# Four raw weight buffers instead of three, and weights joined straight into their buffers, in a fused attention and two-MLP kernel

## The chip, the cores and the metric

The kernel runs on one core of a Trainium2 chip. The metric is the device time of one execution, in microseconds (us). Engines are named as in the profile: PE (TensorE, matmuls), DVE (VectorE), ACT (ScalarE), POOL (GpSimd) and SP (SyncE, which only issues transfers). Each engine works through its own instructions in order.

## What is computed

The weights come out of `setup_inputs` in float64, since they are scaled by a float64 factor; q, k and v are float32. Cut to what matters:

```python
# q, k, v: (4, 8, 576, 64); chunks of 64
scores = scale * q_c @ k_c^T            # per chunk, 64 x 64
attn = softmax(scores); out = attn @ v_c
x = out as 2304 tokens x 512
h = x @ w_in                            # 512 x 2048
x = silu(h) @ w_out                     # 2048 x 512
a, b = x @ w_a, x @ w_b                 # 512 x 1536 each
return (a * b) @ w_out2                 # 1536 x 512; w_o in the kernel
```

## The kernel before

**Weights.** The kernel receives the float64 weights as 64-bit words and makes float32 of them on the chip. There are 68 units of 128 x 512 words (512 KB each): 32 "a" units (`w_in` and `w_out`, 16 each, for the first MLP) and 36 "b" units (`w_a`, `w_b`, `w_o`, 12 each, for the second). One conversion has four steps, each a function: `fetch` (SP transfers the words into a raw buffer, L143), `magnitude` (DVE clamps the high words, L165), `scaled` (ACT makes two passes over the raw buffer, L176 and L178), and `begin` (DVE joins high and low words into a tile `w`, L188, and so frees the raw buffer). The raw buffers are used in turn; there are `RAWS = 3`. `convert` (named "cv" in the orders below) calls `fetch_next` and then `scaled`; `joined` ("af") calls `begin` and then `magnitude`. `fetch_next` issues one fetch if a buffer is free, and then `leave` issues the stores of finished `w` tiles, on SP too.

A joined "a" unit is split into a high part (`upper`, ACT, L210) and a low part (`lower`, DVE, L217), because each product is made of three matmuls in a rounded format (high x high, high x low, low x high). `w_out` units are also stored to HBM (`wo`). A joined "b" unit is stored to HBM as `wf` (36 stores of 256 KB).

**First MLP.** `front` is x @ `w_in` for one of 16 slices m of the hidden width (12 matmuls of 512 columns, then SiLU twice on ACT into `g` and `ghi`, L418, and their difference `glo` on DVE, L416); `back` adds the slice's product with `w_out`. The loop `for k in range(MA)` (the first pass, k = 0 to 15) runs over the slices for the first block of tokens and, beside it, for a side block of 256 tokens, while the weights of the slice after it are converted. The order of the instructions in one iteration is a list of words written out by hand, with "cv" and "af" three times each. The second pass (k = 16 to 31) runs the slices for the second block, with "cv" and "af" twice per iteration; its attention tiles belong to the blocks of the group stage. Then comes the group stage, 32 products `g_front` for the last two blocks, each followed by `g_silu`, and behind them seven rounds of `g_back`.

Attention tiles are spread over the iterations: scores, maximum, exponential, norm, transposes and values of a tile are each put at a fixed word of some iteration. In the first pass four tiles start at k = 2, 5, 8 and 11; scores come at the tile's first iteration, transposes two later and values three later.

**Second MLP.** It uses products of blocks in the manner of Strassen (seven instead of eight), so its weights need sums. The sums for ten units (`w_a`/`w_b` units 0 to 3, and the six `w_o` units) are made ahead ("premade"): `comb_load` and `comb_load_2` bring a unit's two parts from `wf` into a slot `buf` (POOL transfers), `comb_sums` makes the sums (DVE: one of 256, one of 512, one of 256 columns), `comb_high` (ACT) and `comb_low` (DVE) split them, and POOL stores the result (`wg`, `w2`). They are taken from the list `aux_ops`, one step per iteration of the second pass from k = 25 on ("au"), two per product of the group stage. The other eight units are loaded from `wf` and summed later, during the second MLP itself.

**Memory.** The pool `big` has `MA + 4` = 20 slots of 8 KB per partition, for weights, inputs, outputs, `buf` and the split parts. Transfers issued by POOL take their descriptors from a scratch in SBUF; it has 16 KB per partition where the program names no other size.

Of the kernel before, what the change touches and what calls it, by code (L numbers as in the profile page):

```python
# [9 lines left out]
F32 = mybir.dt.float32  # L10
F32R = mybir.dt.float32r
U32 = mybir.dt.uint32
# [4 lines left out]
ALU = mybir.AluOpType  # L17
# [11 lines left out]
def chunk_attention_silu_mlp_gated_mlp(  # L29
# [67 lines left out]

    const = ctx.enter_context(tc.tile_pool(name="const", bufs=1))
    stat = ctx.enter_context(tc.tile_pool(name="stat", bufs=3))
    big = ctx.enter_context(tc.tile_pool(name="big", bufs=MA + 4))  # L100
    gpool = ctx.enter_context(tc.tile_pool(name="gpool", bufs=2))
    spool = ctx.enter_context(tc.tile_pool(name="spool", bufs=2))
    dram = ctx.enter_context(tc.tile_pool(name="dram", bufs=1, space=DRAM))
# [11 lines left out]
        return big.tile([P, 4 * DM], dt, tag="b", name=name)  # L115


    RAWS = 3
    def raw_tile():
        return spool.tile([P, RAWS, DM], U64, tag="raw", name="raws", bufs=1)  # L120

# [30 lines left out]
    def words(raw):  # L152
        w32 = raw.bitcast(U32).rearrange("p (f t) -> p f t", t=2)
        return w32[:, :, 0], w32[:, :, 1]
# [26 lines left out]
    def begin():  # L181

        if not opened:
            return
        dest, raw = opened.pop(0)
        low, high = words(raw)
        w = spool.tile([P, DM], F32, tag="tmp", name="w", bufs=3)
        nc.vector.scalar_tensor_tensor(  # L188
            out=w.bitcast(U32), in0=high, scalar=3, in1=low,
            op0=ALU.logical_shift_left, op1=ALU.bitwise_or,  # L190
        )
        if dest[0] == "f":
            wf[dest[1:]] = d = dram.tile([P, DM], F32, name=f"wf{dest[1]}{dest[2]}")
            leaving.append((d, w))
        else:
            _, m, j = dest
            if j:
                w2h = w.rearrange("p (h n) -> p h n", h=2)
                leaving.append((wo[:, m % 2, :, m // 2], w2h))
            stage_1.append((dest, w))  # L200
# [275 lines left out]
            nc.gpsimd.dma_start(out=buf[:, sl], in_=wf[mat, m].rearrange("p (o n) -> p o n", o=2))  # L476
        bufs[u] = buf

    def comb_load_2(s):

        buf = slot("buf", F32).rearrange("p (o n) -> p o n", o=8)
        for h in range(2):
            nc.gpsimd.dma_start(out=buf[:, 1 - h], in_=wf[2, 2 * s][:, h * H:(h + 1) * H])
        nc.gpsimd.dma_start(
            out=buf[:, 2:8:5], in_=wf[2, 2 * s + 1].rearrange("p (o n) -> p o n", o=2)
        )
        bufs["o", s] = buf

    summed = set()

# [147 lines left out]
        ]  # L638


    units_a = [(m, j) for m in range(MA) for j in range(2)]
    units_b = []
    for s in range(STEPS):
        for mat in range(2):
            units_b += [("f", mat, 2 * s), ("f", mat, 2 * s + 1), ("f", 2, 2 * s + mat)]
    done = [0, 0]

    def next_a():
# [18 lines left out]
    with tc.manual_schedule():  # L667
# [325 lines left out]
        def g_take(s, y):  # L993

            if s == 0:
                g_units[s, y] = [
                    gpool.tile([P, DM], F32R, tag=tg, name="u") for tg in ("ghi", "glo")
                ]
                return
            if y and s > 2:  # L1000
                t = late["gun"].tile([P, 2, DM], F32R, tag=f"u{s}", name="u")
                g_units[s, y] = t[:, 0], t[:, 1]
            elif s < 3 or s > 5:
                if (s, y) not in g_units:
                    t = slot("u").rearrange("p (u t n) -> p u t n", u=2, t=2)
                    pair = ((s, 0), (s, 1)) if s < 3 else ((6, 0), (7, 0))
                    for i, key in enumerate(pair):
                        g_units[key] = t[:, i, 0], t[:, i, 1]
            elif (s, y) not in g_units:
                t = spool.tile([P, 6, DM], F32R, tag="raw", name="u", bufs=1)  # L1010
                for i in range(3):
                    g_units[3 + i, 0] = t[:, 2 * i], t[:, 2 * i + 1]

        def g_front(n):
            m, h = divmod(n, 2)
# [143 lines left out]

        def fetch_next():  # L1160

            if len(fetched) + len(opened) < RAWS:
                fetches[0] += 1
                if done[0] < len(units_a) and fetches[0] % 3:
                    fetch(*next_a())
                elif done[1] < len(units_b):
                    fetch(*next_b())
            leave()

        def convert():  # L1170
# [27 lines left out]
        }  # L1198
        for k in range(MA):
            run(k, "x")  # L1200
            for x in order:
                if x in todo_1:
                    todo_1[x](k)
                else:
                    run(k, x[0])
            run(k, "e")

        aux = [("o", 0), ("o", 1), ("o", 2), 0, ("o", 3), 1, ("o", 4), 2, ("o", 5), 3]

        def aux_load():  # L1210
            if aux:
                u = aux.pop(0)
                (comb_load if u in range(UNITS) else lambda u: comb_load_2(u[1]))(u)
                aux_ops.extend(((comb_sums, u), (comb_high, u, 0), (comb_low, u, 0, 1), (comb_low, u, 1)))

        aux_ops = []

        def comb_high(u, h):
            o0, o1 = HALVES[h]
# [21 lines left out]
        def aux_op():  # L1241
            if not aux_ops:
                return
            f, *args = aux_ops.pop(0)
            if f is comb_sums:
                aux_load()
            f(*args)

        AUX_FROM = MA + 9

        def next_front(k):
            if k + 1 == END:
# [2 lines left out]
            elif k + 1 not in pend:  # L1255
                front(k + 1)

        def aux_step(k):
            if k == AUX_FROM:
                aux_load()  # L1260
            elif k > AUX_FROM:
                aux_op()

        order_2 = (
            "fr a a2 cv c fi af d au ba cv b e af"
        ).split()
        todo_2 = {
            "fr": next_front,
            "cv": lambda k: convert(),
            "af": lambda k: joined(),  # L1270
            "fi": lambda k: finish(pend, k + 1),
            "au": aux_step,
            "ba": lambda k: k in pend and back(k),
        }

# [3 lines left out]
        for k in range(MA, END):  # L1279
            b, m = steps[k]  # L1280
            run(k, "x")
            if k == MA:
                side_cm.__exit__(None, None, None)
                g_cm = tc.tile_pool(name="gate", bufs=1, side="right", reuse_waits="tile")
                late["g"] = g_cm.__enter__()
            for x in order_2:
                if x in todo_2:
                    todo_2[x](k)
                else:
                    run(k, x)  # L1290

        for n, g in enumerate([0, 2, 4, 6, 1, 3, 5, 7] + list(range(8, 4 * SA))):
            if n > 1:
                g_front(g)
            if n == 2:
                run(END, "a")
            if n == 4:
                late.pop("g")
                g_cm.__exit__(None, None, None)
                att_cm.__exit__(None, None, None)  # L1300
                gun_cm = tc.tile_pool(name="gun", bufs=1, side="right", reuse_waits="tile")
                late["gun"] = gun_cm.__enter__()
            g_silu(g)
            if fetched or opened or leaving:
                convert()
                joined()
            if n > 3:
                aux_op()
                aux_op()
            if n == 4 * SA - 12:  # L1310
                w_load("a11")
            if n >= 4 * SA - 3:
                w_chunk(0, n - (4 * SA - 3))
            if n == 4 * SA - 2:
                w_load("a12")
# [260 lines left out]
```

## Time and profile before

| | |
|---|---|
| median of 3 runs | 856.1 us (853.99 to 857.77) |
| the profiled execution's own time | 859.48 us |
| its span, first to last instruction | 857.7 us |
| PE busy | 832.2 us, 97% |
| DVE busy | 550.0 us, 64% |
| ACT busy | 468.4 us, 55% |
| POOL busy | 65.4 us, 8% |
| data moved | 209.59 MB, 244 GB/s in the mean |

Busy time is the time in which an engine executes; waits for other engines are not in it. The profiled execution is one execution, not the median; 1.8 us of its own time lie outside the span.

### The profile page before, as it was taken

Reading aid. Unit: us, or ns where it says so; the run is one execution under the profiler, and the core shown is the slowest. Engines: PE = TensorE matmul, PEld = TensorE weight load, DVE = VectorE, ACT = ScalarE, POOL = GpSimd, SP = SyncE. Lnnn points to the kernel's source line nnn. Section 1 sums busy time; section 2 is a strip of 40 time slices with the busy share of each in tenths; the row PEclk is TensorE's granted clock in tenths of the full one; section 3 lists DMA queues with packets and bytes.
Section 4 is the critical chain, followed back from the end, with each engine's and each line's share of the span. In section 5 each row is a group of like instructions: output and inputs, shape, how many; then the busy total and the mean of one; then the engine's idle time right before and its main releaser. Section 6 shows DMA issues by size and latency. Waiting matters only on the chain.

```text
span 857.7 us, 14083 instructions
## 1 busy us (share of the span) xinstructions
PE 832.2 (97%) x5394; PEld 757.8 (88%) x5394; DVE 550.0 (64%) x972; ACT 468.4 (55%) x900; POOL 65.4 (8%) x118
## 2 busy tenths in 40 slices
PE   7989799898999999999999999999999999999998
PEld 6878688776888888888889999999999999999998
DVE  5656566566763567789885998594454594454563
ACT  6967677767885544465664554373333273333252
POOL 1000000001022123310001110000000000000000
PEclk8999999999999999999999999999999999999999
DMA  8577577779872449982039977888666888666761
GB/s 297 163 233 236 204 244 240 223 253 339 287 256 75 160 160 309 328 316 89 12 106 371 380 304 285 328 300 292 246 254 250 301 339 264 241 252 255 291 236 55
DMA packets 58083, 209.59 MB, mean 244 GB/s; under 512 B 6432, under 2 KB 18336, under 8 KB 48544
## 3 DMA queue, kind: packets, MB, share of 16 engines
q1 hardware_dynamic: 47264, 169.07, 54.8%
q0 software_dynamic: 10464, 39.33, 13.4%
q8 instruction: 42, 0.69, 0.3%
q10 hardware_dynamic: 288, 0.30, 0.1%
q14 instruction: 25, 0.20, 0.1%
HBM read 152.57 MB, written 56.10 MB: 243 GB/s over the span
## 4 chain that ended last, share of the span: by engine, by line
PE 80%; DMA 9%; ACT 5%; DVE 3%; issue 2%; SPq 0%; POOL 0%; DVEq 0%; ACTq 0%
PE ps_acc L897 26%; PE ps_sA L897 8%; PE ps_mm L897 8%; PE ps_sB L897 7%; PE ps_at L897 7%; PE ps_acc L436 6%; DMA raws<-w_out 5%; PE ps_acc L390 5%; PE ps_mm L390 5%; PE ps_sA L390 3%; PE ps_at L390 2%; DMA raws<-w_o 2%; PE ps_sB L390 1%; DVE w L188 1%; ACT raws L178 1%
## 5 line engine op out<-in xcount | busy, mean ns | idle before, releaser
L897 PE MATMUL ps_acc<-xo,ring 128*128 128x384 f32 x902 | 171.9, 334 | 0.0
L897 PEld LDWEIGHTS ps_acc<-xo,ring 128*128 128x128 f32 x902 | 157.7, 188 | 0.4 <-DVE gq L972 0.3
L436 PE MATMUL ps_acc<-ghi,wA 128*128 128x512 f32 x256 | 84.2, 411 | 6.1 <-ACT ghi L418 4.9
L176 ACT ACTIVATE raws<-raws 128x512 int32<-128x512 uint8 x68 | 46.8, 689 | 34.0 <-DMA raws<-w_out 24.9
L390 PE MATMUL ps_mm<-xhi,wA 128*128 128x512 f32 x224 | 61.6, 397 | 0.2
L188 DVE SCALAR_TENSOR_TENSOR w<-raws 128x512 uint32<-128x512 uint32 x68 | 46.8, 689 | 23.0 <-ACT raws L178 21.2
L897 PE MATMUL ps_acc<-u,ring 128*128 128x384 f32 x322 | 61.3, 334 | 0.0
L436 PEld LDWEIGHTS ps_acc<-ghi,wA 128*128 128x128 f32 x256 | 46.8, 194 | 16.4 <-ACT ghi L418 6.2
L1344 ACT ACTIVATE u<-gq 128x384 fp32r<-128x384 f32 x84 | 40.6, 517 | 30.9 <-DVE gq L972 28.5
L897 PEld LDWEIGHTS ps_acc<-u,ring 128*128 128x128 f32 x322 | 56.3, 188 | 0.0
L1345 DVE TENSOR_TENSOR u<-gq,u 128x384 fp32r<-128x384 f32 x84 | 44.4, 552 | 15.2 <-ACT u L1344 15.0
L178 ACT ACTIVATE raws<-raws 128x512 f32<-128x512 f32 x68 | 45.5, 669 | 11.9 <-DVE raws L165 11.7
L436 PE MATMUL ps_acc<-glo,wA 128*128 128x512 f32 x128 | 51.6, 403 | 0.0
L390 PEld LDWEIGHTS ps_mm<-xhi,wA 128*128 128x128 f32 x224 | 40.9, 190 | 8.0 <-PE ps_sB L436 0.6
L165 DVE TENSOR_SCALAR raws<-raws 128x512 f32<-128x512 f32 x68 | 28.8, 423 | 28.4 <-DMA raws<-w_out 21.7
L416 DVE TENSOR_TENSOR glo<-g,ghi 128x512 fp32r<-128x512 f32 (+1 forms) x48 | 28.7, 598 | 26.2 <-ACT ghi L418 26.1
L897 PE MATMUL ps_sA<-xo,ring 128*128 128x384 f32 x220 | 44.4, 334 | 0.0
L906 ACT ACTIVATE gq<-ps_acc 128x384 f32<-128x384 f32 x31 | 15.3, 492 | 52.8 <-PE ps_acc L897 49.7
L897 PE MATMUL ps_mm<-xo,ring 128*128 128x384 f32 x214 | 43.2, 334 | 0.0
L897 PE MATMUL ps_sB<-xo,ring 128*128 128x384 f32 x208 | 42.3, 335 | 0.0
L897 PE MATMUL ps_at<-xo,ring 128*128 128x384 f32 x202 | 41.0, 334 | 0.0
L897 PEld LDWEIGHTS ps_sA<-xo,ring 128*128 128x128 f32 x220 | 38.7, 188 | 0.0
(250 smaller groups left out, 1742.6 us busy)
## 6 DMA issues: line engine op xcount, KB each, us to landing
ring<-w SPq DMA_DIRECT2D x30, 1024.0 KB, 6.4
ring<-wg SPq DMA_DIRECT2D x28, 1024.0 KB, 4.9
ring<-wg SPq DMA_DIRECT2D x28, 768.0 KB, 6.0
wf<-w SPq DMA_DIRECT2D x36, 256.0 KB, 3.7
raws<-w_in SPq DMA_DIRECT2D x16, 512.0 KB, 4.8
raws<-w_out SPq DMA_DIRECT2D x16, 512.0 KB, 4.5
wg<-ring SPq DMA_DIRECT2D x8, 1024.0 KB, 4.6
buf<-wf POOLq DMA_DIRECT2D x26, 256.0 KB, 6.1
```

Source lines behind the costliest of these rows:

```text
L165: nc.vector.tensor_scalar(out=high, in0=high, scalar1=LARGEST, scalar2=-LARGEST, op0=ALU.min, op1=ALU.max)
L176: nc.scalar.activation(low.bitcast(I32), top, AF.Copy, scale=2.0**-5, bias=-31 / 64)
L178: nc.scalar.activation(high, high, AF.Prelu, scale=2.0**-112, alpha=-(2.0**32))
L188: nc.vector.scalar_tensor_tensor(out=w.bitcast(U32), in0=high, scalar=3, in1=low, op0=ALU.logical_shift_left, op1=ALU.bitwise_or,)
L390: nc.tensor.matmul(ps, lhsT=a[:, kk * P:(kk + 1) * P], rhs=b[:, kk, :], start=(j == 0 and kk == 0), stop=(j == 2 and kk == KT - 1),)
L416: nc.vector.tensor_tensor(out=glo, in0=g, in1=ghi.bitcast(F32), op=ALU.subtract)
L436: nc.tensor.matmul(acc_t[b][j], lhsT=a[:, j * P:(j + 1) * P], rhs=g, start=(m == 0 and i == 0 and (b != SIDE or j % 2 == 0)), stop=(m == M ...
L897: nc.tensor.matmul(ps, lhsT=a, rhs=b, start=first and i == 0, stop=last and i == 2, skip_group_check=True,)
L906: nc.scalar.activation(dst, ps, AF.Copy)
L1344: nc.scalar.activation(hi, src, AF.Copy)
L1345: nc.vector.tensor_tensor(out=lo, in0=src, in1=hi.bitcast(F32), op=ALU.subtract)
```

## The change

A fourth raw buffer and a 21st slot are paid for with the POOL scratch, cut from 16 KB to 4 KB per partition (a raw buffer is 4 KB, a slot 8 KB). `fetch_next` may issue two fetches at a call. Every fourth iteration of the first pass leaves its third "cv" and "af" out, the second pass has one of each per iteration instead of two, and products 2 to 19 of the group stage have one each. The 20 "b" units of the premade sums come last in the order of conversion, and `begin` writes them with two joins of 256 columns straight into their places in `buf` (`direct`); they are stored to no `wf` and loaded by no POOL transfer. They may start at k = 22 (`room`).

```diff
-    big = ctx.enter_context(tc.tile_pool(name="big", bufs=MA + 4))
+    big = ctx.enter_context(tc.tile_pool(name="big", bufs=MA + 5))
-    RAWS = 3
+    RAWS = 4
...
         if not opened:
             return
+        if opened[0][0][0] == "d" and not room:
+            return
         dest, raw = opened.pop(0)
         low, high = words(raw)
+
+        def join(out, n=slice(None)):
+            nc.vector.scalar_tensor_tensor(
+                out=out.bitcast(U32), in0=high[:, n], scalar=3, in1=low[:, n],
+                op0=ALU.logical_shift_left, op1=ALU.bitwise_or,
+            )
+
+        if dest[0] == "d":
+            direct(dest, join)
+            return
         w = spool.tile([P, DM], F32, tag="tmp", name="w", bufs=3)
-        nc.vector.scalar_tensor_tensor(
-            out=w.bitcast(U32), in0=high, scalar=3, in1=low,
-            op0=ALU.logical_shift_left, op1=ALU.bitwise_or,
-        )
+        join(w)
...
+    def direct(dest, join):
+
+        _, mat, m = dest
+        s = m // 2
+        u = ("o", s) if mat == 2 else 2 * s + mat
+        if u not in bufs:
+            bufs[u] = slot("buf", F32).rearrange("p (o n) -> p o n", o=8)
+        buf = bufs[u]
+        places = ((1, 0) if mat == 2 else (1, 2), (2, 7) if mat == 2 else (0, 7))[m % 2]
+        for h, o in enumerate(places):
+            join(buf[:, o], slice(h * H, (h + 1) * H))
+        if m % 2:
+            aux_ops.extend(
+                (("sums", u), ("high", u, 0), ("low", u, 0, 1), ("low", u, 1))
+            )
...
-            if len(fetched) + len(opened) < RAWS:
-                fetches[0] += 1
-                if done[0] < len(units_a) and fetches[0] % 3:
-                    fetch(*next_a())
-                elif done[1] < len(units_b):
-                    fetch(*next_b())
+            for _ in range(2):
+                if len(fetched) + len(opened) < RAWS:
+                    fetches[0] += 1
+                    if done[0] < len(units_a) and fetches[0] % 11 not in (0, 3, 6):
+                        fetch(*next_a())
+                    elif done[1] < len(units_b):
+                        fetch(*next_b())
             leave()
...
-            for x in order:
+            for n, x in enumerate(order):
+                if k % 4 == 3 and x in ("cv", "af") and order[:n].count(x) == 2:
+                    continue
...
         order_2 = (
-            "fr a a2 cv c fi af d au ba cv b e af"
+            "fr a a2 cv c fi af d au ba b e"
         ).split()
...
+            if k == MA + 6:
+                room.append(k)
...
-            if fetched or opened or leaving:
+            if 2 <= n < 20:
                 convert()
                 joined()
...
-    nc = bacc.Bacc("TRN2", target_bir_lowering=False, num_devices=1)
+    nc = bacc.Bacc("TRN2", target_bir_lowering=False, num_devices=1, dynamic_dma_scratch_size=4096)
```

PE's instructions keep their order. On SP's queue, at the start of the first pass, these stood behind the loads of `v` (`raws<-...` are fetches, `wo<-w` and `wf<-w` the stores of joined units); before:

```order
L143 DMA raws<-w_out 128x512
L150 DMA wo<-w 128x2x256 x2
L143 DMA raws<-w_in 128x512
L143 DMA raws<-w_a 128x512
L150 DMA wo<-w 128x2x256
L143 DMA raws<-w_out 128x512
L143 DMA raws<-w_in 128x512
L150 DMA wf_726<-w 128x512
```

And now:

```order
L143 DMA raws<-w_out 128x512
L143 DMA raws<-w_in 128x512
L150 DMA wo<-w 128x2x256 x2
L143 DMA raws<-w_a 128x512
L143 DMA raws<-w_out 128x512
L143 DMA raws<-w_in 128x512
L150 DMA wo<-w 128x2x256
```

One more fetch stands ahead of the stores of the first joined units, and so on through the pass: each fetch has moved ahead by one conversion.

On DVE, in the iterations k = 26 and 27 of the second pass, from one `glo` to the next (the `sm`, `rs` and `s` rows are the norm of an attention tile, `buf<-buf` the sums); before:

```order
L416 TENSOR_TENSOR glo<-g,ghi 128x512
L494 TENSOR_TENSOR buf<-buf 128x256
L495 TENSOR_TENSOR buf<-buf 128x512
L501 TENSOR_TENSOR buf<-buf 128x256
L313 TENSOR_REDUCE sm<-s 128x8
L314 TENSOR_SCALAR sm<-sm 128x8
L318 RECIPROCAL rs<-sm 128x8
L323 TENSOR_TENSOR s<-s,rs 128x2x4x64
L416 TENSOR_TENSOR glo<-g,ghi 128x512
```

And now, with the line numbers of the changed kernel:

```order
L425 TENSOR_TENSOR glo<-g,ghi 128x512
L191 SCALAR_TENSOR_TENSOR buf<-raws 128x256 x2
L165 TENSOR_SCALAR raws<-raws 128x512
L1241 TENSOR_TENSOR hl<-buf,hl 128x3x256
L322 TENSOR_REDUCE sm<-s 128x8
L323 TENSOR_SCALAR sm<-sm 128x8
L327 RECIPROCAL rs<-sm 128x8
L332 TENSOR_TENSOR s<-s,rs 128x2x4x64
L425 TENSOR_TENSOR glo<-g,ghi 128x512
L191 SCALAR_TENSOR_TENSOR buf<-raws 128x256 x2
L165 TENSOR_SCALAR raws<-raws 128x512
```

Each of the two iterations has the two joins of a unit and a `magnitude` there now, and a part of a split (`hl`) stands in the first; the three sums follow in the second.

## Rows read from the trace of the kernel before

**Rows 1.** The page, its first line: span and instructions.

```profile
span 857.7 us, 14083 instructions
```

**Rows 2.** Waits of PE, whole span: who for whom, us in total, times, longest.

```profile
PE ps_at L261 <- ACT ghi L418: 6.0, 3, 3.2
PE ps_acc L436 <- ACT ghi L418: 4.9, 2, 3.3
...
PE ps_acc L436 <- DVE y L455: 1.1, 1, 1.1
```

**Rows 3.** Windows: length, busy us (instructions) by engine, granted clock, DMA share, GB/s.

```profile
core 0: us, PE busy (x) PEld busy (x) DVE busy (x) ACT busy (x) POOL busy (x), PEclk, DMA share, GB/s
35.05:188.69 153.64, 140.62 (x989) 118.88 (x987) 93.98 (x191) 111.74 (x204) 5.89 (x11) 0.97 0.70 228
188.69:217.00 28.31, 25.02 (x192) 19.81 (x191) 18.20 (x40) 21.37 (x37) 5.37 (x10) 0.94 0.96 339
...
301.00:386.00 85.00, 85.00 (x406) 70.15 (x406) 62.73 (x85) 43.01 (x72) 23.78 (x37) 1.00 0.79 281
```

**Rows 4.** Timeline of PE, first matmuls of front(4), (5), (6), (9), (10): start, us.

```profile
65.87 0.85 PE L390 MATMUL ps_mm<-xhi,wA 128*128 128x512 f32 x3
...
74.56 0.63 PE L390 MATMUL ps_mm<-xhi,wA 128*128 128x512 f32 x2
...
83.38 0.86 PE L390 MATMUL ps_mm<-xhi,wA 128*128 128x512 f32 x3
...
118.60 0.86 PE L390 MATMUL ps_mm<-xhi,wA 128*128 128x512 f32 x3
...
128.28 0.86 PE L390 MATMUL ps_mm<-xhi,wA 128*128 128x512 f32 x3
```

**Rows 5.** Waits of ACT, 35.05 to 217 us.

```profile
ACT raws L176 <- DMA raws<-w_out: 24.9, 12, 4.8
...
ACT raws L176 <- DMA raws<-w_b: 2.9, 1, 2.9
```

**Rows 6.** Timeline, pieces of five engines; in brackets the idle time before, and its end.

```profile
91.76 0.54 POOL L250 DMA_DIRECT2D v<-v  x1 [9.94 <-PE ps_mm L261]
...
91.97 0.41 SPq L143 DMA_DIRECT2D raws<-w_out  x1
...
100.43 0.70 ACT L176 ACTIVATE raws<-raws 128x512 int32<-128x512 uint8 x1 [3.27 <-DMA raws<-w_out]
...
104.13 0.79 PE L436 MATMUL ps_acc<-ghi,wA 128*128 128x512 f32 x1 [3.28 <-ACT ghi L418]
...
104.72 0.68 DVE L188 SCALAR_TENSOR_TENSOR w<-raws 128x512 uint32<-128x512 uint32 x1
...
106.50 0.69 DVE L188 SCALAR_TENSOR_TENSOR w<-raws 128x512 uint32<-128x512 uint32 x1 [0.42 <-ACT raws L178]
...
108.29 0.69 DVE L188 SCALAR_TENSOR_TENSOR w<-raws 128x512 uint32<-128x512 uint32 x1 [0.16 <-ACT raws L178]
...
209.73 0.68 ACT L176 ACTIVATE raws<-raws 128x512 int32<-128x512 uint8 x1 [4.09 <-DMA raws<-w_o]
...
211.49 0.27 PE L261 MATMUL ps_at<-k,q 64*64 64x64 f32 x1 [2.16 <-ACT pt L336]
```

**Rows 7.** The line that fetches (L143), 35 to 189 us.

```profile
DMA to landing us min/median/max: 3.7/4.8/8.4
```

**Rows 8.** Windows: a pair of iterations with four conversions, one with none.

```profile
229.70:242.40 12.70, 12.70 (x118) 10.36 (x117) 9.11 (x21) 11.18 (x20) 1.59 (x3) 1.00 0.86 290
255.10:267.80 12.70, 12.70 (x118) 10.36 (x117) 5.14 (x13) 6.81 (x12) 3.37 (x7) 1.00 0.35 107
```

**Rows 9.** Groups by line, 188 to 400 us: busy us, mean ns, idle before.

```profile
L188 DVE SCALAR_TENSOR_TENSOR w<-raws 128x512 uint32<-128x512 uint32 x20 | 13.8, 689 | 7.2 <-ACT raws L178 7.2
...
L1227 DVE TENSOR_TENSOR hl<-buf,hl 128x1024 fp32r<-128x1024 f32 x10 | 12.2, 1218 | 0.7 <-ACT hl L1221 0.7
...
L494 DVE TENSOR_TENSOR buf<-buf 128x256 f32<-128x256 f32 x10 | 4.2, 420 | 1.1 <-DMA buf<-wf 0.8 <-issue 0.2
...
L1221 ACT ACTIVATE hl<-buf 128x1024 fp32r<-128x1024 f32 x10 | 10.6, 1060 | 33.2 <-DVE buf L495 33.2
```

More of the change, by code (lines that the diff above doesn't have):

```diff
@@ L477, in comb_load @@
         bufs[u] = buf
[L479 to L487, printed above, removed]
+    def direct(dest, join):
[12 more added lines that the diff above has]
+            )
     summed = set()
@@ L638, in operands @@
         ]
+    aux_ops = []
+    room = []
     units_a = [(m, j) for m in range(MA) for j in range(2)]
[L642 to L645, printed above, removed]
+    units_b = [
+        ("f", mat, 2 * s + i)
+        for s in range(EARLY // 2, STEPS) for mat in range(2) for i in range(2)
+    ]
+    for u in (0, ("o", 0), 1, ("o", 1), ("o", 2), 2, ("o", 3), ("o", 4), 3, ("o", 5)):
+        s, mat = divmod(u, 2) if u in range(UNITS) else (u[1], 2)
+        units_b += [("d", mat, 2 * s), ("d", mat, 2 * s + 1)]
     done = [0, 0]
@@ L1002, in g_take @@
                 g_units[s, y] = t[:, 0], t[:, 1]
-            elif s < 3 or s > 5:
+            elif s < 5:
                 if (s, y) not in g_units:
                     t = slot("u").rearrange("p (u t n) -> p u t n", u=2, t=2)
-                    pair = ((s, 0), (s, 1)) if s < 3 else ((6, 0), (7, 0))
+                    pair = ((s, 0), (s, 1)) if s < 3 else ((3, 0), (4, 0))
                     for i, key in enumerate(pair):
@@ L1011, in g_take @@
                 for i in range(3):
-                    g_units[3 + i, 0] = t[:, 2 * i], t[:, 2 * i + 1]
+                    g_units[5 + i, 0] = t[:, 2 * i], t[:, 2 * i + 1]
         def g_front(n):
@@ L1206, in chunk_attention_silu_mlp_gated_mlp @@
             run(k, "e")
[L1208 to L1216, printed above, removed]
         def comb_high(u, h):
@@ L1244, in aux_op @@
             f, *args = aux_ops.pop(0)
[L1245 to L1249, printed above, removed]
+            {"sums": comb_sums, "high": comb_high, "low": comb_low}[f](*args)
         def next_front(k):
@@ L1256, in next_front @@
                 front(k + 1)
[L1258 to L1262, printed above, removed]
         order_2 = (
-            "fr a a2 cv c fi af d au ba cv b e af"
+            "fr a a2 cv c fi af d au ba b e"
         ).split()
@@ L1271, in chunk_attention_silu_mlp_gated_mlp @@
             "fi": lambda k: finish(pend, k + 1),
-            "au": aux_step,
+            "au": lambda k: aux_op(),
             "ba": lambda k: k in pend and back(k),
```

## The prediction

> **What bounds the kernel now.** I read the page first: the execution spans 857.7 us [rows 1]. Then the waits of TensorE: the largest are for ScalarE's SiLU results, `ps_at` and `ps_acc` behind `ghi` [rows 2]. Then the busy times by stretch, to see where they lie. From 301 to 386 us (the group stage) TensorE is busy 85.00 of 85.00 us, but in the first pass over the weights (35.05 to 188.69 us) 140.62 of 153.64, and in the 28.31 us behind it 25.02 [rows 3]. So what can be won is in the first 217 us; behind them TensorE's own stream is the bound, and the change leaves that stream as it is.
>
> Next, how long an iteration k of that pass must be. The stretch of 153.64 us runs from the first matmul of front(1) to that of front(16): 15 iterations, 10.24 us on average. Those without a stall show what TensorE needs [rows 4]: 74.56 - 65.87 = 8.69 us for a plain one, 83.38 - 74.56 = 8.82 with the transposes of an attention tile, 128.28 - 118.60 = 9.68 with the scores and the values of tiles.
>
> What holds the others up: ScalarE waits for fetched raw weights. Of its waits from 35 to 217 us, 24.9 us are for `w_out` fetches, 12 times, and 2.9 for one of `w_b` [rows 5]; one of 4.09 us for `w_o` comes at 209.73 [rows 6]. One case shows the chain [rows 6]: SP issues a `w_out` fetch at 91.97; ScalarE has waited 3.27 us for it when it starts at 100.43; the SiLU stands behind that on ScalarE, and TensorE resumes at 104.13 after 3.28 us of idleness. The granted clock then falls too: its mean over the pass is 0.97 of full speed, which for a clock of two levels (2.4 and 1.2 GHz) is about 9 us at the lower [rows 3].
>
> Why is it always the fetch of `w_out`? Each conversion is fetch, `magnitude` (VectorE), `scaled` (ScalarE), `begin` (VectorE, the join). `magnitude` of one unit stands right behind the join of the unit before it, and with three buffers a fetch starts when the join three units back has freed its buffer. So a fetch has the time from one join to the next but one. In an iteration the joins stand close together, at 104.72, 106.50 and 108.29 [rows 6]. For the first unit of the next iteration that time is 108.29 - 104.72 = 3.57 us; for the other two, with iterations of 8.8 us, 8.8 - 1.78 and 8.8 - 1.79, 7.0 us each. Fetches land 3.7 to 8.4 us after issue, 4.8 in the median [rows 7]. 3.57 us is less than the fastest of them: the first unit waits in nearly every iteration, the others hardly ever, and the waits that add up [rows 5] are just so.
>
> **The change, part by part.**
>
> *Fourth raw buffer.* A fetch now starts when the join four units back is done, so it has the time of three steps between joins: with three units per iteration, a whole iteration, 8.7 to 9.7 us, for each of the three. Against a landing of 4.8 us and a wait of as much as 1 us in SP's queue (its issues take 0.41 us each [rows 6]) that leaves 3 us; the longest, 8.4 us, would be late by less than one. ScalarE's wait should go almost wholly. What it is worth, with clean lengths in place of the real ones: six plain iterations of 8.69 (52.1), four with transposes of 8.82 (35.3), three with scores and values of 9.68 (29.0), two with scores or values alone, which I put halfway at 9.2 (18.4). Sum 134.8 against 153.64: **18.8 us**.
>
> *The 28.31 us behind it.* TensorE idles 3.29 us there [rows 3]; 1.1 is for the copy of `y` [rows 2], which stays. The other 2.2 are TensorE's wait up to 211.49, right behind ScalarE's 4.09 us for `w_o` [rows 6], and the clock, 0.94 in the mean, is about 3.4 us at the lower level and so 1.7 us lost. Together **3.9 us**.
>
> *Four conversions fewer in the pass* (in every fourth iteration the third is left out), and two fetches where one buffer more is free. ScalarE is busy 111.74 and VectorE 93.98 of the 153.64 us [rows 3]. A conversion costs ScalarE (11.18 - 6.81) / 4 = 1.1 us and VectorE (9.11 - 5.14) / 4 = 1.0, from a pair of iterations with four of them and one with none [rows 8]. So 107 and 90 us would be left for some 135: ScalarE at 80%. That is not the bound, but in an iteration with an exponential and its two table loads it can be late by a microsecond or so. I take **2.7 us** for such rests over both stretches; the bounds are nothing, and half of the gain (a rival below).
>
> *Joins straight into the buffers.* 20 units lose a store to HBM and a load from it on POOL's queue; nothing on TensorE waited for either, so by themselves they are worth nothing. Two joins of 256 columns replace one of 512: 2 x 0.420, from the subtraction of that width, against 0.689 [rows 9], 0.15 us more each, 3 us of VectorE in all. What hides it, and the conversions that now come later: in the second pass (k = 16 to 31) a pair of iterations of 12.70 us had up to 9.11 us of VectorE and 11.18 of ScalarE, and TensorE was busy all the time [rows 8]. Afterwards, from k = 22 on, a full pair holds two conversions, one set of sums and about one split: VectorE 5.14 + 2 x 1.0 + 2 x 0.15 + 1.53 (two of 256 columns, one of 512) + 1.22 = 10.2, ScalarE 6.81 + 2 x 1.1 + one or two splits of 1.06 = 10.1 to 11.1 [rows 8, 9]. For ScalarE that is a load already seen without a stall, for VectorE 1.1 us more with 2.5 to spare. In the group stage VectorE goes from 62.73 to 62.73 + 10 x 1.15 less some 3.7 that the new order moves ahead of it, 70 of 85 us. So: **nothing**. Without this cover each microsecond above 12.70 in a pair would be one on the end, in five pairs.
>
> *New waits.* The first join into a slot can wait until that slot's former content has left. Behind a late join on VectorE stand the norm of the softmax and `glo`, and behind those TensorE. No trace of before shows it. From below it is nothing, from above a transfer's longest landing, 8.4 us [rows 7], once per unit; the slot's former transfer is issued an iteration or more earlier, and there is one slot more, so I take nothing.
>
> *The smaller scratch.* It holds the descriptors of POOL's transfers; nothing of before shows a wait for room in it. From below it costs nothing; the upper bound is a rival. I take nothing, since POOL has little under way at once.
>
> **Sum.** 18.8 + 3.9 - 2.7 = 20.0 us. The profiled execution's own time is 859.5 us, so it would take 839.5; it lies 3.4 us above the median of the runs, 856.1. For the median that gives **836 us**.
>
> **A rule against it.** The fetch of 91.97 took over 8 us to be used, and the fastest of all took 3.7 [rows 6, 7]. The Trainium skill, in "DMA: Bandwidth & Descriptors", section "Anatomy of one DMA — SWDGE (gpsimd) path", fits a transfer's time as 2.0 us and its bytes over 436 GB/s. That is measured on POOL's path and not on SP's; for a fetch of 512 KB it makes an estimate of 3.2 us. By it 3.57 us would nearly do, three buffers would be enough and the fourth worth nothing. The trace differs (4.8 in the median), and the measurement decides. What the kernel would do by it is the third rival.
>
> **The rivals.**
> 1. *Half of it.* More fetches under way share the same DMA engines, which are at 0.70 in the pass and 0.96 behind it [rows 3], and each lands later; or ScalarE, in order, is late anyway in the iterations with exponentials. For it: the fetch of 91.97, more than 8 us on its way, ran beside POOL's load of `v`, issued 0.2 us before it [rows 6]. Against it: the units with 7.0 us hardly waited. If half of ScalarE's wait stays, the gain is about 10 us: 846.
> 2. *Slower.* POOL's transfers wait for room in a scratch of a quarter of the size. In the second pass a pair of iterations needs three loads (q, k, v) and up to two stores there. One after another, at the 4.8 us of a fetch, they take 24 us where a pair has 12.70, and the scores wait: 11 us in each of the five pairs with stores, 55 in all, and 856 + 55 - 20 = 891. It decides from the point where less than two transfers fit; against it stands that these are few and large.
> 3. *No change.* A lone fetch (3.7 us) is nearly in time with three buffers; only bunches are late. With a deeper queue the bunch is one larger, its last fetch as late as before, and TensorE's wait only moves to another unit: 856, within 3. Against it: the second and third of a bunch hardly waited.
> 4. *More.* The 2.7 us and some of the short gaps go as well: below 829.
>
> **Chances and range.** My forecast (829 to 842) 0.66, half (842 to 851) 0.18, more 0.05, no change 0.05, slower 0.06. Runs of this kernel can tell about 0.5% (4.3 us) from no change. Faster by more than that is 0.66 + 0.18 + 0.05 = 0.89, the same 0.05, slower 0.06. The range takes in the forecast and most of the half, and a little of what is better: 828 to 850.
>
> **What would show it.** Right: ScalarE's waits for `w_out` in the first pass fall from 24.9 us to under 5; front(1) to front(16) takes 135 to 139 us; the clock stays at full speed in it; behind it (from 217 us before, then from some 195) TensorE stays without a gap; POOL's loads from `wf` are left for the eight later units alone. Wrong: waits of ScalarE for VectorE's `magnitude` in place of the fetches; landings of fetches over 8 us in most iterations; TensorE waiting for the transposes' input or for a bank in the second pass or the group stage; POOL's loads of q and k issued late.

## The result

The changed kernel takes **835.85 us** in the median of 4 runs (835.26 to 836.49); the kernel before, in 4 runs, 856.12. The ratio is 0.9765, 95% interval [0.9742, 0.9788]. The forecast was 836.

The first three lines are from the page of the changed kernel (span, busy time, granted clock in 40 slices).

```profile
span 834.2 us, 13965 instructions
...
PE 825.7 (99%) x5394; PEld 753.5 (90%) x5394; DVE 549.5 (66%) x992; ACT 471.2 (56%) x900; POOL 49.6 (6%) x92
...
PEclk8999999999999999999999999999999999999999
```

Windows of the changed kernel follow, with the columns of [rows 3]: front(1) to front(16), the stretch behind it, five pairs of iterations of the second pass (the first of them without conversions), and 85 us of the group stage.

```profile
35.34:170.33 134.99, 134.99 (x988) 115.19 (x987) 90.21 (x185) 111.02 (x200) 5.92 (x11) 1.00 0.79 244
170.33:193.42 23.09, 23.09 (x192) 18.72 (x191) 11.99 (x28) 16.06 (x29) 5.38 (x10) 1.00 0.69 230
...
206.11:218.79 12.68, 12.68 (x117) 10.35 (x116) 5.12 (x13) 6.80 (x12) 1.60 (x3) 1.00 0.20 62
218.79:231.48 12.69, 12.69 (x118) 10.35 (x116) 8.17 (x21) 7.38 (x13) 1.61 (x3) 1.00 0.40 129
231.48:244.17 12.69, 12.69 (x118) 10.35 (x117) 8.19 (x20) 10.48 (x18) 2.14 (x4) 1.00 0.70 221
244.17:256.85 12.68, 12.68 (x117) 10.35 (x116) 9.37 (x23) 9.02 (x16) 2.14 (x4) 1.00 0.67 233
256.85:269.54 12.69, 12.69 (x118) 10.35 (x116) 8.19 (x20) 10.49 (x18) 1.30 (x2) 1.00 0.61 197
...
277.42:362.42 85.00, 85.00 (x406) 70.17 (x406) 68.64 (x107) 52.83 (x88) 12.09 (x18) 1.00 0.72 266
```

In every row the busy time of TensorE is the length of the window. The first pass went from 153.64 to 134.99 us, the stretch behind it from 28.31 to 23.09, and the granted clock is 1.00 in both (0.97 and 0.94 in [rows 3]).

The waits of ScalarE in the changed kernel, 30 to 217 us (answering to [rows 5]), and the landing times of the fetches, 35 to 170 us (to [rows 7]):

```profile
ACT g L427 <- PE ps_mm L399: 16.2, 12, 2.2
ACT raws L178 <- DVE raws L165: 8.5, 14, 1.5
ACT g L427 <- PE ps_at L399: 4.6, 12, 0.7
...
DMA to landing us min/median/max: 3.7/4.9/6.5
```

No wait for `w_out` is listed any more. ScalarE now waits mostly for TensorE, as it should where TensorE is the bound. In the median a fetch lands no sooner than before (4.9 us against 4.8; the longest takes 6.5 against 8.4); it is asked for sooner ahead of its use.

### The profile page after: what moved, and what is told of

Same layout as the page of the kernel before. It is cut to its first block, busy times and chain, and to the rows that moved or that the text cites. A ratio compares the mean times of both kernels' runs of the same rounds, so it can differ in the third digit from the quotient of the medians.

```text
span 834.2 us, 13965 instructions
## 1 busy us (share of the span) xinstructions
PE 825.7 (99%) x5394; PEld 753.5 (90%) x5394; DVE 549.5 (66%) x992; ACT 471.2 (56%) x900; POOL 49.6 (6%) x92
## 4 chain that ended last, share of the span: by engine, by line
PE 97%; ACT 1%; DMA 1%; DVE 0%; SPq 0%; issue 0%; POOL 0%
PE ps_acc L917 27%; PE ps_acc L445 11%; PE ps_mm L399 9%; PE ps_sA L917 8%; PE ps_mm L917 8%; PE ps_sB L917 7%; PE ps_at L917 7%; PE ps_acc L399 5%; PE ps_at L399 4%; PE ps_sA L399 4%; PE ps_sA L445 1%; PE ps_sB L445 1%; PE ps_sB L399 1%; PE ps_at L270 1%; DMA start<-kt 1%; PE ps_at L341 1%
## 5 line engine op out<-in xcount | busy, mean ns | idle before, releaser
L445 PE MATMUL ps_acc<-ghi,wA 128*128 128x512 f32 x256 | 81.6, 400 | 0.0
L191 DVE SCALAR_TENSOR_TENSOR w<-raws 128x512 uint32<-128x512 uint32 x48 | 33.1, 690 | 18.8 <-ACT raws L178 10.9
L917 PEld LDWEIGHTS ps_mm<-xo,ring 128*128 128x128 f32 x214 | 37.6, 188 | 0.0
```

The lines of the kernel that those rows point to most:

```text
L191: nc.vector.scalar_tensor_tensor(out=out.bitcast(U32), in0=high[:, n], scalar=3, in1=low[:, n], op0=ALU.logical_shift_left, op1=ALU.bitwis ...
L445: nc.tensor.matmul(acc_t[b][j], lhsT=a[:, j * P:(j + 1) * P], rhs=g, start=(m == 0 and i == 0 and (b != SIDE or j % 2 == 0)), stop=(m == M ...
L917: nc.tensor.matmul(ps, lhsT=a, rhs=b, start=first and i == 0, stop=last and i == 2, skip_group_check=True,)
```

## Where the late fetch came from

The prediction put the gain down to the fourth raw buffer. The first experiment refuted that, so here are the rows that show what made the fetch late. The kernel before, 45 to 58 us, timelines of SP's queue, of VectorE and of ScalarE:

```profile
45.66 0.37 SPq L143 DMA_DIRECT2D raws<-w_a  x1
49.88 0.38 SPq L150 DMA_DIRECT2D wo<-w  x1
50.31 0.46 SPq L246 DMA_DIRECT2D q<-qt  x1
50.82 0.44 SPq L246 DMA_DIRECT2D k<-kt  x1
51.37 0.36 SPq L143 DMA_DIRECT2D raws<-w_out  x1
...
49.17 0.69 DVE L188 SCALAR_TENSOR_TENSOR w<-raws 128x512 uint32<-128x512 uint32 x1
...
58.00 0.70 ACT L176 ACTIVATE raws<-raws 128x512 int32<-128x512 uint8 x1 [4.81 <-DMA raws<-w_out]
```

SP's queue was served in the order of the program. The fetch of `w_out` stands there behind the store of a joined unit, which waits for that join (it ends at 49.86), and behind the loads of `q` and `k`. With three buffers the same join frees the buffer that this fetch takes, so its place costs it little here: it goes out 1.51 us after the join's end. ScalarE starts 6.63 us after its issue.

In the other iterations nothing but the store stands between, and the fetch goes out 0.5 us after the join. The 13 fetches of `w_out` from 42 to 167 us go out 0.6 us after the join in the mean and land in 5.3 us (3.8 to 8.4). The prediction's 3.57 us from one join to the next but one cannot cover that.

The old `fetch_next` makes one fetch at a call and puts it ahead of that call's store; the next fetch belongs to the next call, and so stands behind the store. With one fetch and one join in turn the number under way never grows: a third buffer, or a fourth, is not filled ahead.

## The experiments

The kernel before was run again beside each batch (medians 853.4 to 854.4 us); every ratio is to those runs, with its 95% interval. The result's own ratio is to other runs (856.12 us).

| edit | us | ratio |
|---|---|---|
| fourth buffer, small scratch | 854.06 | 1.0006 [0.9976, 1.0036] |
| changed kernel, three buffers | 836.09 | 0.9811 [0.9796, 0.9827] |
| small scratch alone | 852.91 | 0.9994 [0.9976, 1.0011] |
| changed kernel, scratch of 1 KB | 835.57 | 0.9776 [0.9748, 0.9804] |
| changed kernel, premade units through HBM | 851.66 | 0.998 [0.9963, 0.9997] |
| changed kernel, direct joins three times | 851.47 | 0.996 [0.9943, 0.9976] |
| one join earlier in the order | 839.96 | 0.9826 [0.9798, 0.9853] |
| filling rule alone, three buffers | 839.27 | 0.9832 [0.9785, 0.988] |
| filling rule, four buffers, small scratch | 837.03 | 0.9803 [0.9748, 0.9857] |
| changed kernel, old filling rule | 842.05 | 0.9859 [0.9813, 0.9906] |
| q and k loads by POOL | 852.2 | 0.9982 [0.9947, 1.0017] |
| stores by POOL | 851.11 | 0.997 [0.9946, 0.9994] |

### The fourth buffer alone

```diff
-    RAWS = 3
+    RAWS = 4
-    nc = bacc.Bacc("TRN2", target_bir_lowering=False, num_devices=1)
+    nc = bacc.Bacc("TRN2", target_bir_lowering=False, num_devices=1, dynamic_dma_scratch_size=4096)
```

> The kernel before with four raw buffers and the scratch of 4 KB that pays for them; order of conversions, joins and slots as before. Theory (a fetch has the time from the join four units back): ScalarE's waits for w_out in the first pass fall from 24.9 us to under 5, front(1) to front(16) takes 135 to 138 us, time 836 to 840. Rival (the lighter first pass or the direct joins bring the gain): the waits may go, but ScalarE with all 48 conversions is late, and the time is 848 to 856.

No change: 1.0006. Its timelines of SP's queue and ScalarE at the same place, its row of ScalarE's waits, 30 to 217 us, and one join on VectorE:

```profile
49.97 0.38 SPq L150 DMA_DIRECT2D wo<-w  x1
50.39 0.46 SPq L246 DMA_DIRECT2D q<-qt  x1
50.90 0.44 SPq L246 DMA_DIRECT2D k<-kt  x1
51.44 0.38 SPq L143 DMA_DIRECT2D raws<-w_out  x1
...
56.60 0.69 ACT L176 ACTIVATE raws<-raws 128x512 int32<-128x512 uint8 x1 [3.32 <-DMA raws<-w_out]
...
ACT raws L176 <- DMA raws<-w_out: 21.4, 12, 3.3
...
44.70 0.69 DVE L188 SCALAR_TENSOR_TENSOR w<-raws 128x512 uint32<-128x512 uint32 x1
```

The buffer that this fetch takes was emptied by the join that starts at 44.70 and ends at 45.39. Still the fetch goes out at 51.44, as before, 6 us later. What held it was not the buffer but its place in the queue, behind the store that waits for the next join (49.25). The wait of 21.4 us is no sign of a gain: the kernel before with the small scratch alone has 19.1 us in 11 waits in its profiled execution (853.33 us), where [rows 5] has 24.9 in one of 859.48 us.

### The changed kernel with three buffers

```diff
-    RAWS = 4
+    RAWS = 3
```

> The changed kernel with three raw buffers; all else as changed (direct joins, conversions spread further, 21 slots, small scratch). Theory: the time from one join to the next but one is back, so ScalarE waits again for fetches in most iterations of the first pass, 15 us or more; the iterations with two conversions and the second pass are relieved, so the time is 845 to 853. Rival (the spread brings the gain): 836 to 840.

The gain stays (0.9811; 836.09 us against 835.85 with four buffers), and with it the first pass: 135.46 us. So the fourth buffer is not needed in the changed kernel either. ScalarE's waits for `w_out` are 3.8 us, 5 times; none of TensorE's is listed there.

### The filling rule alone, and with a fourth buffer

```diff
-            if len(fetched) + len(opened) < RAWS:
-                fetches[0] += 1
...
+            for _ in range(2):
+                if len(fetched) + len(opened) < RAWS:
+                    fetches[0] += 1
...
```

> The kernel before with the new filling rule alone (fetch_next may issue two fetches at a call); three buffers, order of conversions and slots as before. New theory, after the fourth buffer alone did nothing and three buffers in the changed kernel lost nothing: before, only two of the three buffers are ever filled ahead in program order, so each fetch stands in SP's queue behind the store of the unit whose join it waits for, and behind q and k loads; with the rule it stands ahead of them. Then ScalarE's waits for w_out fall from 24.9 us to under 8, front(1) to front(16) takes 135 to 142 us, time 837 to 845. Rival (the four conversions fewer in the first pass are what counts): 850 to 857.

> The kernel before with the new filling rule, four buffers and the scratch of 4 KB. New theory: with the rule the fourth buffer is filled, a fetch has the time from the join four units back, and ScalarE's waits for w_out fall to under 2 us; time 836 to 842, at or a little below that with three. Rival (the four conversions fewer count): 848 to 857.

Both as expected. The kernel before with this rule alone, SP's queue and ScalarE at the same place:

```profile
49.71 0.33 SPq L143 DMA_DIRECT2D raws<-w_out  x1
50.09 0.43 SPq L150 DMA_DIRECT2D wo<-w  x1
50.56 0.47 SPq L246 DMA_DIRECT2D q<-qt  x1
51.07 0.47 SPq L246 DMA_DIRECT2D k<-kt  x1
...
54.90 0.70 ACT L176 ACTIVATE raws<-raws 128x512 int32<-128x512 uint8 x1 [1.10 <-DMA raws<-w_out]
```

The fetch now stands ahead of the store and goes out at 49.71, 1.66 us earlier; ahead of `q` and `k`, ScalarE has it 5.19 us after its issue instead of 6.63. The wait falls from 4.81 to 1.10 us.

Over the 13 fetches of `w_out` in the pass the mean time from the join's end to the issue falls from 0.6 us to 0.07, and the landing from 5.3 us to 4.4. (In the run with the small scratch alone they are 0.6 and 4.8.) ScalarE's waits for them are 7.3 us, 10 times; the first pass takes 136.24 us. So with three buffers the fetch gains little time in the queue, about half a microsecond, and as much or more in the landing. That it lands sooner because no store was issued just ahead of it is likely; no run tries that alone.

With the fourth buffer as well the rule reaches a whole unit further. Each `w_out` fetch then goes out within 0.1 us of the join four units back, no wait for `w_out` is listed, and the first pass is as long as in the changed kernel:

```profile
34.22:169.23 135.01, 135.01 (x989) 115.20 (x987) 92.97 (x191) 114.70 (x206) 5.88 (x11) 1.00 0.86 260
```

Between 839.27 and 837.03 the intervals overlap, so the fourth buffer's 2 us under the new rule are likely, not shown. Nor is this last version told apart from the changed kernel (0.9803 against 0.9765, overlapping).

### The changed kernel with the old filling rule

```diff
-            for _ in range(2):
+            for _ in range(1):
```

> The changed kernel with one fetch at a call as before; four buffers, direct joins, conversions spread further, 21 slots. New theory: each fetch stands behind the store of a joined unit again, and ScalarE waits for fetches, 10 us or more in the first pass; time 843 to 853. Rival (the spread brings the gain by itself): 835 to 838.

842.05, a little better than expected. The rest of the change therefore brings some 11 us without the filling rule; since the fourth buffer alone brings nothing, the fewer conversions in the pass and the other order of units are the likely part, not shown. What is left is the old wait, 8.3 us in 5 times (30 to 217 us), and 6.4 us more in 4 waits for `w_in` and `w_a`:

```profile
ACT raws L176 <- DMA raws<-w_out: 8.3, 5, 3.7
```

The two parts overlap: 14 us for the rule alone, 11 without it, and with both some 18, counted from the same runs of the kernel before (853.37; the 20 of the result is counted from 856.12). They remove the same lateness.

### One join earlier

```diff
-            "cv ba1 sb fr af sf ba0 N2 lw up cv si fi ss T2 S0 af V3 cv X3 up sfi P2 M0 L3 E0 af lw"
+            "cv ba1 sb fr af sf ba0 N2 lw up cv af si fi ss T2 S0 V3 cv X3 up sfi P2 M0 L3 E0 af lw"
```

> The kernel before, three buffers, with one word moved: the second of the three joins of an iteration (and the magnitude behind it) stands right behind its conversion, ahead of the SiLU and the difference glo, and not behind the scores. Theory (the time between joins decides): that join comes some 2.5 to 3 us earlier, its buffer's next fetch has 6 us or more in place of 3.57, and another fetch's time shrinks from 7.0 to about 4 us; the waits for w_out fall to under half of 24.9 us, a part of them comes back at another fetch, time 845 to 854. Rival (the fetches are late because of their bunching and the load on the DMA engines): the waits stay at 20 us or more in all, time 854 to 858.

839.96: one word moved in the order of the kernel before, with three buffers and the old rule, takes 14.4 us off, more than either theory gave it. ScalarE's waits for `w_out` fall to 4.5 us, 5 times. Each `w_out` fetch of the pass still stands behind its store and goes out 0.5 us after the join (1.53 once), so with three buffers the store in front is not what counts most: the time from that join to the use is, as the prediction had read it.

### q and k, or the stores, on POOL's queue

```diff
-            at(k - 1, "e", lambda: load_qk(i, A, nc.gpsimd if o else nc.sync))
+            at(k - 1, "e", lambda: load_qk(i, A))
```

> The kernel before with the q and k loads of the first tile of the pass issued by POOL, not by SP, where they stand ahead of the fetch issued at 51.37 us. New theory: that fetch is issued 1 us earlier, ScalarE's wait for it falls from 4.8 us to 2 to 3.5 and TensorE's idle time of 3.2 us behind it to under 2; the later ones stay in the main, time 849 to 855 against some 854. Rival (that first late fetch sets off all the later ones): ScalarE's waits for w_out under 8 us, time 836 to 842.

Inconclusive: 852.2, its runs from 845.23 to 856.65. The fetch goes out 1 us earlier (50.38), ScalarE's wait for it falls to 1.56 us and TensorE's wait behind it is gone. In this profile (an execution of 847.37 us, near the lower end of its runs) ScalarE's waits for `w_out` are 13.5 us instead of 19.1 to 24.9. So these loads may have a part in it, but the time does not clearly follow.

```diff
-            nc.sync.dma_start(out=dst, in_=src)
+            nc.gpsimd.dma_start(out=dst, in_=src)
```

> The kernel before, three buffers and the old filling rule, but the stores of the joined units (wo, wf) are issued by POOL and no longer by SP, where each fetch stood behind one. If a fetch is late because it stands in SP's queue behind a store that waits for a later join, it now goes out as soon as its buffer is free: ScalarE's waits for w_out in the first pass fall from 24.9 us to 3 to 9, front(1) to front(16) takes 135 to 141 us, 838 to 846 us in all. Rival, that too few fetches are under way whatever stands between them in the queue (or that a fetch lands too late anyway): the waits stay at 20 us or more, 850 to 857 us. POOL's loads of v, q and k then stand behind those stores, which can take back some 5 us in either case.

Half a hit. Waits of three engines in the kernel with stores on POOL, 30 to 217 us:

```profile
ACT raws L176 <- DMA raws<-w_out: 6.3, 9, 1.0
...
DVE w L188 <- DMA wf<-w: 10.9, 7, 2.8
...
PE ps_sA L436 <- DVE glo L416: 4.0, 4, 1.8
PE ps_at L261 <- DMA k<-kt: 3.2, 2, 1.7
```

With the stores out of SP's queue, and nothing else changed, the waits for `w_out` fall from 24.9 to 6.3 us, inside the 3 to 9 that the queue gives and far from the rival's 20. The fetches go out 0.06 us after the join and land in 4.4 us in the mean. But the first pass falls only to 145.6 us, not 135 to 141, and the time to 851.11, where the rival had put it. The rest went into new waits: VectorE's join waits for its output tile, whose last store to `wf` is not done, TensorE for `glo` behind that join (4.0 us), and for `k`, which POOL now issues behind a store (3.2 us). That is more than the 5 us I had set aside for POOL.

### The premade units through HBM again

```diff
+        w = spool.tile([P, DM], F32, tag="tmp", name="w", bufs=3)
+        join(w)
+        wf[mat, m] = d = dram.tile([P, DM], F32, name=f"wf{mat}{m}")
+        leaving.append((d, w))
+        leave()
...
-        for h, o in enumerate(places):
-            join(buf[:, o], slice(h * H, (h + 1) * H))
...
+                nc.gpsimd.dma_start(out=buf[:, 1 - h], in_=d[:, h * H:(h + 1) * H])
...
+            nc.gpsimd.dma_start(out=buf[:, sl], in_=d.rearrange("p (o n) -> p o n", o=2))
```

> The changed kernel, but the 20 units of the premade sums go through HBM as before: joined into a w tile in one piece, stored by SP, loaded into their slot by POOL, and a unit's sums are queued one unit later. Theory: the direct joins by themselves are worth nothing, 834.5 to 838. Rival: the store, the load and the landing between them cost TensorE a wait in the second pass or the group stage, 840 or more.

The rival came, not the theory: nearly the whole gain is lost (0.998), and not in the first pass, which stays clean (134.99 us). The waits of TensorE from 217 to 420 us, and the timelines of POOL and ScalarE ahead of it:

```profile
PE ps_at L399 <- ACT u L1071: 7.2, 1, 7.2
...
331.86 1.09 POOL L503 DMA_DIRECT2D buf<-wf  x2 [6.32 <-DMA wf<-w]
332.94 0.76 POOL L1263 DMA_DIRECT2D w<-hl  x1
...
337.24 0.60 ACT L1071 ACTIVATE u<-ps_at 128x512 fp32r<-128x512 f32 x1 [5.15 <-DMA w<-hl]
```

The same thing happens on another queue: POOL's load from `wf` waits 6.32 us for the store to land, behind it stands the transfer of the finished split (`w<-hl`), for that ScalarE waits, and TensorE for ScalarE. That wait and 2.4 us in two other places make 9.6 of the 12.4 us between the two spans (846.6 and 834.2); behind the long one the granted clock was at its lower level (1.2 GHz) for some microseconds: from 330 to 345 us its mean is 0.77.

### The direct joins three times

```diff
-            join(buf[:, o], slice(h * H, (h + 1) * H))
+            for _ in range(3):
+                join(buf[:, o], slice(h * H, (h + 1) * H))
```

> The changed kernel with each direct join done three times over the same places, so that VectorE has 1.7 us more per conversion in the second pass and the group stage. By the sums of the prediction a full pair of iterations then holds 10.2 + 2 x 1.7 = 13.6 us of VectorE where TensorE needs 12.70, and the group stage 70 + 17 = 87 of 85. Theory (VectorE covers the joins with 2.5 us per pair to spare): TensorE waits in the second pass, 838 to 846. Rival (the room is larger, since the start of the group stage takes up what is late): 835 to 837.

It cost 15.6 us (851.47), not the few that were expected. Windows of four of its stretches, a piece of VectorE's timeline, and TensorE's longest wait from 217 to 420 us:

```profile
219.33:232.02 12.69, 12.69 (x118) 10.35 (x116) 11.48 (x29) 7.38 (x13) 1.61 (x3) 1.00 0.40 128
232.02:244.71 12.69, 12.69 (x118) 10.35 (x117) 11.50 (x28) 10.46 (x18) 2.13 (x4) 1.00 0.47 176
244.71:261.86 17.15, 14.12 (x118) 11.30 (x116) 12.76 (x31) 9.14 (x16) 2.14 (x4) 0.90 0.59 207
302.00:343.00 41.00, 34.72 (x151) 27.82 (x150) 39.55 (x78) 17.32 (x27) 4.72 (x7) 0.98 0.58 218
...
247.63 2.60 DVE L191 SCALAR_TENSOR_TENSOR buf<-raws 128x256 uint32<-128x256 uint32 x6 [2.56 <-DMA wg<-hl]
...
PE ps_sB L399 <- ACT gy L1054: 4.8, 1, 4.8
```

Two pairs of 12.69 us hold 11.5 us of VectorE, and TensorE does not notice: up to there the cover is as summed. In the third pair a join waits 2.56 us for a transfer out of its slot (`wg<-hl`), issued at 242.12 here and at 239.32 in the changed kernel, and TensorE then loses 3.03 us (17.15 - 14.12), with the clock at 0.90 in the mean. VectorE's own work in that pair, 12.76 us, is just over the 12.69 as well, so the slot wait takes most of the loss there. The larger part is lost in the group stage: from 302 to 343 us VectorE is busy 39.55 of 41.00 us, ScalarE waits for its sums and TensorE for ScalarE, 6.28 us in all (41.00 - 34.72). There it is VectorE's time that is full, as the expectation had it. The two make 9.3 of the 15.2 us between the spans (849.4 and 834.2), and the lower clock behind them a part of the rest.

### The scratch

```diff
-    nc = bacc.Bacc("TRN2", target_bir_lowering=False, num_devices=1)
+    nc = bacc.Bacc("TRN2", target_bir_lowering=False, num_devices=1, dynamic_dma_scratch_size=4096)
```

> The kernel before with the scratch of 4 KB and nothing else. Theory: POOL's transfers never fill it, 854 to 858, POOL's transfers land in 4 to 7 us as before. Rival (they wait for room): over 860, POOL's loads of q and k issued late.

```diff
-dynamic_dma_scratch_size=4096)
+dynamic_dma_scratch_size=1024)
```

> The changed kernel with a scratch of 1 KB in place of 4 KB. Theory (POOL has little under way at once): a quarter still holds what is under way, 834.5 to 837.5. Rival (transfers wait for room below some size): POOL's issues stretch from 0.54 us to some microseconds, its transfers land later, 840 or more.

The first is the kernel before with the small scratch (0.9994), the second the changed one with a smaller one still (0.9776, against 0.9765 with 4 KB). Neither moves.

## Why the prediction was right, and where it was not

**The bound and its size: right.** ScalarE's wait for `w_out` fetches was what made the first pass long, and the iterations have the clean lengths: 134.99 us against the 134.8 of the sum.

**"Fourth raw buffer": the step that failed.** It reads "A fetch now starts when the join four units back is done", as if a free buffer were enough. But the fetch also waits for its place in SP's queue, and with one fetch at a call that place is behind the store of the unit three back, which waits for its join. With four buffers and the old rule the fetch of 51.44 went out 6 us after its buffer was free, as late as before, and nothing was gained (1.0006). The rule of two fetches at a call, which I named only in passing, is what makes that sentence true: with it every `w_out` fetch of the first pass goes out within 0.1 us of the join four units back, in the changed kernel too. And even then the time does not need the fourth buffer (836.09 us with three). The 18.8 us (18.65 measured) thus belong to the filling rule (14 us of the time when alone) and to what else was changed in the pass (11 us without the rule), not to the buffer.

What the prediction said of the kernel before holds: with three buffers a fetch starts when the join three units back has freed its buffer, to within 0.5 us (1.5 us once), and 3.57 us are too few for landings of 3.8 to 8.4. The join moved by one word shows the same.

**The stretch behind: 5.22 instead of 3.9.** The copy of `y` that "stays" (1.1 us) no longer holds TensorE up either.

**The rests of 2.7 us: did not come.** ScalarE at 111 of 134.99 us (82%) costs TensorE nothing, exponentials and table loads included.

**The sum.** In profiled executions 859.48 to 835.99 is 23.5 us, not 20.0: the two terms above were 1.3 and 2.7 us too cautious, and some 0.5 went elsewhere. The subtraction of 3.4 for an execution above the median made up for it, by chance: it took that excess to stay, but the profiled execution of the changed kernel lies at its median (835.99 against 835.85), and its runs within 1.2 us where those of the kernel before spread over 3.8. The 836 is thus right in its large term and exact by two errors that cancel.

**Direct joins and slots at nothing: right as far as it goes.** A full pair holds 8.2 to 9.4 us of VectorE (10.2 forecast) and 7.4 to 10.5 of ScalarE (10.1 to 11.1), and the group stage 68.6 of 85 us of VectorE (70 forecast); TensorE never waits. But the joins are no free extra: with conversions this late, the way through HBM loses 15.8 us. The joins done three times show both limits that were named: in the second pass the slot wait, priced at nothing, comes as soon as the cover is used up, and in the group stage VectorE's time runs full.

**The rivals.** *Slower* by the scratch: refuted by two runs. *Half*: landings are 4.9 us in the median with more fetches under way, no later. *No change* is exactly what the fourth buffer does alone, though not by a longer bunch. The Trainium skill, in "DMA: Bandwidth & Descriptors", section "Anatomy of one DMA — SWDGE (gpsimd) path", gave an estimate of 3.2 us for a fetch, by which the fourth buffer would have been worth nothing: the figure is not what these fetches show (3.7 to 6.5 us), but its consequence held, for another reason. *More* did not come.

**Left open.** How much of the 11 us without the filling rule is the fewer conversions and how much the changed order of units was not tried apart, nor why the fetches land sooner where no store stands ahead of them, nor what a queue used by nothing but fetches would give.

## What to carry to other kernels

Before you price another buffer, look at what stands ahead of the transfer in its queue: a free buffer is worth nothing to a fetch that is issued behind a store waiting for an engine. And where the buffer itself comes free late, even half a microsecond in the queue, with as much in the landing, counts when it is paid in every iteration: issuing the next fetch before that store, or moving the join that frees the buffer, brought 14 us here with one line or one word, while moving the stores to another queue took most of that wait away and brought others. And test each part alone: a total that comes out to the microsecond did not show which part had made it.

## What was not expected of the hardware

The scratch for the descriptors of POOL's transfers could be cut to 4 KB and to 1 KB without any time lost (852.91 against 853.86, and 835.57 against 835.85). And VectorE can wait for the end of stores: 10.9 us in 7 times with the stores on POOL's queue, 9.3 us in 6 times with the new rule, four buffers and the stores on SP, and 0.9 us, once, in the kernel before. It is thus no matter of POOL's queue alone. In the changed kernel, where it costs TensorE nothing, that wait is 6.7 us, 5 times:

```profile
DVE w L191 <- DMA wf<-w: 6.7, 5, 1.9
```
